# An attention kernel with a two-layer network behind it: ten and six tiles in two output halves, sums of q a unit ahead, and later places for some copies and adds

## The chip, the core and the metric

One Trainium2 chip, one of its cores. TensorE (PE) multiplies matrices, VectorE (DVE), ScalarE (ACT) and GpSimd (POOL) work on tiles, SyncE (SP) issues DMAs; each runs its own instructions in order, and semaphores join them. The metric is the device time of one execution in microseconds (us). Six runs of the kernel before gave 412.99 to 417.33, with a median of 413.75. Durations in the text come from one further execution with the profiler on.

## What is computed

```python
# q, k, v: (8, 12, 448, 64); x: (3584, 768); w_in: (768, 2048); w_out: (2048, 768)
q_n, k_n = rmsnorm(q, g_q), rmsnorm(k, g_k)
scores = matmul(q_n, k_n.transpose(0, 1, 3, 2)) / sqrt(64)
attn = exp(scores - max(scores)); attn = attn / (sum(attn) + 1e-9)
x = matmul(attn, v).transpose(0, 2, 1, 3).reshape(8 * 448, 768)
h = x @ w_in
out = maximum(0.01 * h, h) @ w_out
```

## The kernel before

**Units.** Attention runs in 24 units: 8 batches of 3 groups of 4 heads. For unit u, in this order and spread over several units' time: load q and k (`load`, by SP) and v (`load_v`, by GpSimd's queue); squares (`prep_sq` on ScalarE or `prep_sqp` on GpSimd, L148 and L152); their sums (`prep_ssq`, VectorE, L159); the reciprocal root in two small ScalarE steps (`prep_rinv`, L164 and L165); the normalised q and k in half precision (`prep_norm`, VectorE, L171); a transpose into qkT, on TensorE with VectorE copies for the first units (L753, L755) and by a DMA on SP's queue afterwards (`prep_trd`, L183); and then g's factor (`prep_g`, L155).

**A unit's own time** has four steps d. Step 0 scores column tile 0 (`score`, L199), steps 1 to 3 two tiles each. In step 0 VectorE takes the maximum (`shift_max`, L236) and builds dg (L238); TensorE then finishes the previous unit (products with v, L367, sums of exponentials, L307), and the two shift matmuls (L248) spread dg to all partitions; VectorE reduces them (L249) into the bias eb (L257), which every exponential of the unit needs (L218, ScalarE). Two slots in PSUM hold scores; each is free again when its exponential has been taken. The sums of exponentials are inverted by ScalarE (L327, L332), spread by four DMAs (rz, L337), and multiplied into x, by GpSimd (`xmul_pool`) or VectorE (`xmul_sb`), both at L347.

**The network** fills TensorE between the steps. `queue` holds its items, and `PLAN` says how many of them `fill` takes in each step. `moe1` makes one tile of 128 of the 2048 hidden columns from six matmuls (L389) and ScalarE's leaky step (L383). `moe2` makes half an output tile (384 columns) in two items of eight matmuls each (L435), copies it out of PSUM (VectorE, L439), and after the second half stores it (L409). From the second batch on, pairs of output tiles are made with seven products in place of eight (`seven`, items i0 to i6, L476): ma, mb, mc and md are PSUM banks, `sa` and `tw` hold sums of rows and of weights (`s1` to `s4`, `weight_sum`), and VectorE adds the products into the output tile (L483). i4 makes the fourth product in md, and i6 goes on accumulating in the same bank.

**What sets the order.** The program order is the order on each engine. `later` puts a step into `pend`; the next item's `flush` emits it. `fill` also emits one of the step's `jobs` (loads, sums, normalisation, transpose) after each item, and what is left of them at its end; in step 2 it skips that after an item that is marked `merges` (i4). At the end of step 3 `flush` keeps only s1 to s4 back, which come behind the next unit's maximum.

**The opening** (units 0 to 2, to about 43 us) is written out by hand, with `warm` matmuls between the steps. **The tail** multiplies the last batch's tiles; there (`mixed`) i0 puts half of mb's matmuls between ma's.

```python
flush(keep=d == 3 and u < NU - 1)          # at the end of fill
for i in range(8 * part, 8 * part + 8):    # moe2: two items of eight
```

Of the kernel before, what the change touches and what calls it, by code (L numbers as in the profile page):

```python
# [14 lines left out]
ds = bass.ds  # L15
# [3 lines left out]
def kernel(  # L19
# [11 lines left out]
    nc = tc.nc  # L31
# [6 lines left out]
    NU = B * NQ  # L38
# [28 lines left out]
    def drop(bank):  # L67
        if held:
            held[0].append(bank)
# [342 lines left out]
    pend = []  # L412
    L, R, LR = slice(0, HC), slice(HC, DM), slice(0, DM)

    def flush(keep=False):
        kept = [p for p in pend if keep and p[0] in (s1, s2, s3, s4)]
        now = [p for p in pend if p not in kept]
        pend[:] = kept
        for fn, args in now:
            fn(*args)  # L420
# [1 line left out]
    def out_tile():  # L422
        return opool.tile([P, DM], FP32, tag="ost", name="ost")

    def moe2(pair, t, half, part, late=False):
        flush()
        if half == 0 and part == 0:
            ost[0] = out_tile()
        if part == 0:
            ost[1] = aux([P, 512], FP32, "op2")  # L430
        op2 = ost[1]
        fts = (0, 1, 2, 3, 4, 5, 8, 9, 10, 12, 13, 11, 14, 15, 6, 7) if late else range(FT)
        for i in range(8 * part, 8 * part + 8):
            ft = fts[i]
            nc.tensor.matmul(op2[:, 0:HC], gt[:, ft, ds(col(t), P)], wout16[:, ft, ds(HC * half, HC)],  # L435
                             start=(i == 0), stop=(i == FT - 1))
        if part == 0:
            return
        nc.vector.tensor_copy(ost[0][:, ds(HC * half, HC)], op2[:, 0:HC])  # L439
        drop(op2)  # L440
        if half == 1:
            store(pair, t, ost[0], LR, False)

    def wblock(i, j):
        return wout16[:, HF * i:HF * i + HF, HC * j:HC * j + HC]
# [25 lines left out]
    def seven(pair, tt, nxt=None, last=False, mixed=False):  # L471
        g = {}

        def mm(bank, a, b, first, fs=range(HF)):
            for f in fs:
                nc.tensor.matmul(bank[:, 0:HC], a[:, f], b[:, f], start=(first and f == 0), stop=(f == HF - 1), skip_group_check=not first)  # L476

        def bank(name):
            g[name] = aux([P, 512], FP32, name)
            return g[name]  # L480

        def add(dst, src, name):
            nc.vector.tensor_tensor(dst, g[name][:, 0:HC], src, op=ALU.add)  # L483

        def put(i, c):
            store(pair, tt[i], g["o"][i], c, last)

        def i0():
            flush()
            g["o"] = (out_tile(), out_tile())  # L490
            ma = bank("ma")
            if mixed:
                mm(ma, gblock(tt[0], 0), wblock(0, 0), True, range(6))
                mm(bank("mb"), sa[:, 1], tw[:, 1], True, range(4))
            mm(ma, gblock(tt[0], 0), wblock(0, 0), True, range(6 if mixed else 0, HF))
            later(lambda: nc.vector.tensor_copy(g["o"][1][:, L], g["ma"][:, 0:HC]))

        def i1():
            flush()
            mm(g["mb"] if mixed else bank("mb"), sa[:, 1], tw[:, 1], True, range(4 if mixed else 0, HF))  # L500
            later(lambda: add(g["o"][1][:, L], g["o"][1][:, L], "mb"))
            later(lambda: drop(g["mb"]))

        def i2():
            flush()
            mm(g["ma"], gblock(tt[0], 1), wblock(1, 0), False)
            later(lambda: nc.scalar.copy(g["o"][0][:, L], g["ma"][:, 0:HC]))
            later(lambda: drop(g["ma"]))
            if last:
                later(put, 0, L)  # L510

        def i3():
            flush()
            mm(bank("mc"), sa[:, 0], tw[:, 0], True)
            later(lambda: add(g["o"][1][:, R], g["o"][1][:, L], "mc"))
            if nxt:
                later(s1, nxt)

        def i4():
            flush()  # L520
            mm(bank("md"), sa[:, 2], tw[:, 2], True)
            later(lambda: add(g["o"][1][:, R], g["o"][1][:, R], "md"))
            if last:
                later(put, 1, R)

        i4.merges = True

        def i5():
            flush()
            mm(g["mc"], sa[:, 3], wblock(1, 1), False)  # L530
            if nxt:
                later(s2, nxt)
            later(lambda: add(g["o"][0][:, R], g["o"][1][:, L], "mc"))
            later(lambda: drop(g["mc"]))
            later(put, 0, R if last else LR)
            if nxt:
                later(s3, nxt)
                later(s4, nxt)

        def i6():  # L540
            flush()
            mm(g["md"], gblock(tt[1], 1), tw[:, 3], False)
            later(lambda: add(g["o"][1][:, L], g["o"][1][:, L], "md"))
            later(lambda: drop(g["md"]))
            later(put, 1, L if last else LR)

        return [i0, i1, i2, i3, i4, i5, i6]

# [136 lines left out]
    def push(b):  # L685
        pair, odd = divmod(b, 2)
        fast = b > 0
        order = [f // 2 + HF * (f % 2) for f in range(FT)] if odd else range(FT)
        items = [(1.13, lambda ft=ft: (flush(), moe1(b, ft))) for ft in order]
        half = [(slice(0, 4)), (slice(4, 8))]  # L690
        late = b >= LATE
        after = {}
        if late:
            if odd:
                tt = (3, 4)
                for ns, f in (((1, 3), s1), ((4, 2), s2), ((3, 2), s3), ((5, 3), s4)):
                    after[ns] = [lambda f=f: f(tt, half[0])]
                after[3, 3] = [lambda f=f: f(tt, half[1]) for f in (s1, s2)]
            else:
                after[6, 2] = [lambda: win_sum(1, 0, (raws, "rq", 3))]  # L700
                after[1, 3] = [lambda: win_sum(2, 0, (raws, "rk", 3))]
                after[5, 2] = [lambda: win_sum(4, 0, (prep_p, "n16", 1))]
            item = late1(b, odd, after)
            fts = [0, 8, 1, 9, 2, 10, 3, 11]
            items = []
            for w in (LATE_ALL if odd else LATE_HALF):
                if w == "M":
                    items.append((1.13, lambda ft=fts.pop(0): (flush(), moe1(b, ft))))
                else:
                    items.append((0.575, lambda w=w: item(*w)))  # L710
        if odd:
            tt, tn = (3, 4), (5, 6)
            items += [(1.31, fn) for fn in seven(pair, tt, tn, mixed=late)]
            for n, x, fs in ((len(items) - 7, 1, (s3, s4)),) if late else ((8, 0, (s1, s2)), (10, 0, (s3, s4)), (FT - 1, 1, (s1, s2)), (FT, 1, (s3, s4))):
                c, fn = items[n]
                items[n] = (c, also(fn, *[lambda f=f, x=x: later(f, tt, half[x]) for f in fs]))
            items += [(1.31, fn) for fn in seven(pair, tn, None, b == B - 1)]
        else:
            tiles = (2,) if fast else (0, 1, 2)
            std = [lambda t=t, h=h, p=p: moe2(pair, t, h, p, late) for t in tiles for h in range(2) for p in range(2)]  # L720
            if fast:
                tt = (0, 1)
                std[0] = also(std[0], lambda: later(s1, tt), *[lambda: later(win_sum, 3, 0)] * late)
                std[1] = also(std[1], lambda: later(s2, tt))
                std[2] = also(std[2], lambda: later(s3, tt), lambda: later(s4, tt))
                std += seven(pair, tt)
            items += [(1.31, fn) for fn in std]
        queue.extend(items)
# [12 lines left out]
    def fill(u, d, jobs):  # L741
        for n in range(int(PLAN[u - 3][d])):
            fn = queue.pop(0)[1]
            fn()
            if jobs and not (d == 2 and hasattr(fn, "merges")):
                jobs.pop(0)()
        flush(keep=d == 3 and u < NU - 1)
        for job in jobs:
            job()

# [20 lines left out]
    with tc.manual_schedule():  # L771
# [72 lines left out]
        load(4)  # L844
        gate(1)
        prep_sqp(2, (1,))
        load_w_in(1024, 1024)
        wb = aux([P, 512], FP32, "warm")
        warm(12, wb)
# [9 lines left out]
        k1 = []  # L859
        tr(1, 1, ((K1, lambda *a: k1.append(a)),), tpk)  # L860
        score0(1)
        shift_max(1)
        vcopy(*k1[0])
        shift_bank(1)
# [4 lines left out]
        ex(0)  # L869
        warm(4, st[1]["pb"])  # L870
        shift_mm(1)
        prep_ssq(2)
        ex(1)
        qk(1, (1,))
        ex(1)
        zsum_slot(0)
        pv(0)
        prep_rinv(2)
        zinv(0)
        prep_norm(2)  # L880
        gate(2)
        prep_sqp(3)
        load_v(3)
        load(5)
        prep_sqp(4, (0,))
# [19 lines left out]
        shift_bank(2)  # L905
        warm(12, st[2]["pb"])
        shift_mm(2)
        prep_ssq(3)
        ex(2)
        qk(2, (1,))  # L910
        ex(2)
        zsum_slot(1)
        pv(1)
        prep_rinv(3)
        zinv(1)

        prep_norm(3)
# [11 lines left out]
        warm(8, st[2]["pb"])  # L929
        trn(3, 1, vcopy)  # L930
        xmul(1)
        prep_ssq(4)
        qk(2, (4,))
        ex(2)
        st[2]["zt"] = [aux([P, 512], FP32, "zt") for r in range(2)]
# [158 lines left out]
```

## Time and profile before

| | us |
|---|---|
| median of six runs | 413.75 |
| the profiled execution | 414.25 |
| its span, first to last instruction | 412.5 |
| TensorE busy | 398.2 |
| VectorE busy | 306.8 |
| ScalarE busy | 298.5 |
| GpSimd busy | 68.4 |
| DMA qkT<-n in the chain that ended last | 3.4% of the span |

The granted TensorE clock was 0.998. In the views, a row of the timeline has its start and length in us, the engine and line, the tile written and those read, the shape, a count of like instructions, and in brackets how long the engine was idle before, and for whom. The chain of waits is followed back from the last instruction, at each step to what released it.

### The profile page before, as it was taken

To read this page: it belongs to the slowest core of one execution; us is meant where nothing else is said; L and a number is where in the kernel's file an instruction comes from. 1 tells how busy PE (TensorE), PEld (TensorE's weight loads), DVE (VectorE), ACT (ScalarE), POOL (GpSimd) and SP (SyncE) were. 2 spreads that over 40 slices of the span, in tenths; PEclk is the share of its full clock that TensorE was granted. 3 is DMA by queue.
4 is the path that set the end of the run, shared out by engine and by line. 5 is a ranking of instruction groups with operands and counts; after the bars stand their busy time and mean duration, and the time that the engine had idled before them with its cause. 6 is when DMAs were issued, how large, how long until landed. Compare 5 with 4: busy or idle time off the path is not lost.

```text
span 412.5 us, 9399 instructions
## 1 busy us (share of the span) xinstructions
PE 398.2 (97%) x3840; PEld 219.1 (53%) x3840; DVE 306.8 (74%) x490; ACT 298.5 (72%) x470; POOL 68.4 (17%) x70
## 2 busy tenths in 40 slices
PE   8689999899999999999999999999999999999996
PEld 7445454454445544455445544454445557558953
DVE  5888889987988756767669757678568788658762
ACT  6898977577887689777986679966986657653600
POOL 1868442200020200020020200002001202000000
PEclk9999999999999999999999999999999999999999
DMA  6999999998565895577665796666562470032014
GB/s 205 276 237 252 242 229 247 209 181 187 147 157 86 220 236 106 156 195 162 157 152 80 211 208 138 164 145 158 186 114 46 121 151 17 9 78 76 2 40 114
DMA packets 72526, 62.87 MB, mean 152 GB/s; under 512 B 36388, under 2 KB 67620, under 8 KB 72484
## 3 DMA queue, kind: packets, MB, share of 16 engines
q1 hardware_dynamic: 61888, 50.08, 46.8%
q0 software_dynamic: 10272, 11.80, 18.8%
q8 instruction: 30, 0.49, 0.5%
q10 hardware_dynamic: 324, 0.39, 0.3%
q14 instruction: 12, 0.10, 0.1%
HBM read 45.61 MB, written 11.01 MB: 137 GB/s over the span
## 4 chain that ended last, share of the span: by engine, by line
PE 78%; DVE 10%; DMA 5%; ACT 3%; issue 2%; SPq 1%; DVEq 0%; ACTq 0%
PE hps L389 28%; PE sT L199 8%; PE sT L367 5%; PE bank L602 5%; PE bank L476 5%; PE mc L476 5%; PE ma L476 5%; PE md L476 4%; DMA qkT<-n 3%; DVE n L171 3%; PE op L435 2%; PE mb L476 2%; PE zc L307 2%; PE sT L476 1%; PE bank L435 1%
## 5 line engine op out<-in xcount | busy, mean ns | idle before, releaser
L218 ACT ACTIVATE et<-sT,eb 128x896 f16<-128x896 f32 x166 | 159.5, 1010 | 25.3 <-DVE eb L257 12.7
L389 PE MATMUL hps<-xt,win 128*128 128x448 f16 x600 | 120.8, 353 | 0.0
L389 PEld LDWEIGHTS <-win 128*128 128x128 f16 x612 | 56.7, 98 | 57.9 <-issue 9.9
L383 ACT ACTIVATE gt<-hps 128x448 f16<-128x448 f32 x100 | 53.8, 557 | 3.8 <-PE hps L389 3.2
L199 PE MATMUL sT<-qkT 64*64 64x448 f16 x664 | 52.5, 363 | 3.0 <-ACT et L218 2.1
L159 DVE TENSOR_REDUCE ssq<-sq 128x14 f32<-128x896 f32 (+2 forms) x49 | 50.1, 1058 | 0.6 <-ACT sq L148 0.6
L476 PEld LDWEIGHTS <-sa 128*128 128x128 f16 x352 | 32.8, 98 | 26.4 <-issue 5.8
L128 POOL DMA_DIRECT2D vt<-in_v_dram x24 | 17.9, 746 | 168.0 <-PE sT L367 167.7
L322 ACT COPY x<-sT 128x896 f32<-128x896 f32 x16 | 14.5, 906 | 30.0 <-DVE sT L249 30.0
L476 PEld LDWEIGHTS <-gt 128*128 128x128 f16 x264 | 25.3, 98 | 18.4 <-issue 2.1
L199 PEld LDWEIGHTS <-qkT 64*64 64x64 f16 x672 | 15.3, 104 | 36.1 <-issue 31.7
L347 POOL TENSOR_TENSOR xt<-x,rz 128x896 f16<-128x896 f32 x9 | 18.8, 2090 | 81.4 <-DMA rz<-zs 73.2
L367 PE MATMUL sT<-et,vt 64*64 64x448 f16 x560 | 29.9, 349 | 0.0
L171 DVE TENSOR_TENSOR n<-rq,rinv 128x896 f16<-128x896 f32 (+2 forms) x25 | 27.1, 1088 | 3.0 <-ACT rinv L165 3.0
L236 DVE TENSOR_REDUCE sT<-sT 128x1 f32<-128x896 f32 x22 | 24.1, 1094 | 6.2 <-PE sT L199 6.1
L435 PE MATMUL op<-wout,gt 128*128 128x384 f16 x160 | 28.4, 327 | 0.0
L292 DVE TENSOR_TENSOR ea<-ea,et 128x896 f16<-128x896 f16 x25 | 15.6, 625 | 14.4 <-ACT et L218 13.4
L171 DVE TENSOR_TENSOR n<-rk,rinv 128x896 f16<-128x896 f32 (+2 forms) x26 | 26.1, 1011 | 0.0
L367 PEld LDWEIGHTS <-vt 64*64 64x64 f16 x672 | 20.1, 107 | 10.8 <-issue 0.4
L435 PEld LDWEIGHTS <-gt 128*128 128x128 f16 x192 | 17.7, 98 | 13.7 <-issue 3.1
L476 PE MATMUL ma<-wout,gt 128*128 128x384 f16 x128 | 23.5, 326 | 0.0
L292 DVE TENSOR_TENSOR ea<-et 128x896 f16<-128x896 f16 x14 | 9.4, 672 | 11.4 <-ACT et L218 11.4
(144 smaller groups left out, 547.4 us busy)
## 6 DMA issues: line engine op xcount, KB each, us to landing
rq<-in_q_dram SPq DMA_DIRECT2D x24, 448.0 KB, 4.0
rk<-in_k_dram SPq DMA_DIRECT2D x24, 448.0 KB, 5.2
out_dram<-ost SPq DMA_DIRECT2D x52, 192.0 KB, 3.4
rz<-zs SPq DMA_DIRECT2D x80, 112.0 KB, 2.3
vt<-in_v_dram POOLq DMA_DIRECT2D x24, 224.0 KB, 5.6
win<-in_moe_w_in_dram POOLq DMA_DIRECT2D x8, 384.0 KB, 14.7
wout<-in_moe_w_out_dram POOLq DMA_DIRECT2D x2, 1536.0 KB, 27.8
out_dram<-ost SPq DMA_DIRECT2D x4, 96.0 KB, 2.1
```

The source lines that it names most:

```text
L159: nc.vector.tensor_reduce(buf(u, "ssq")[:, ti, :, c[0]:c[1]], buf(u, f"sq{ti}")[:, :, c[0]:c[1]], axis=AXL.X, op=ALU.add)
L171: nc.vector.tensor_tensor(buf(u, "n16")[:, ti, c[0]:c[1]].rearrange("p s a d -> p a s d"), src[:, :, c[0]:c[1]], buf(u, "rinv")[:, ti, :, ...
L199: nc.tensor.matmul(banks[a][64 * r:64 * r + 64, 0:S].rearrange("p (t x) -> p t x", t=NS), kT(u, r, a, t), qT(u, r, a), start=True, stop=True)
L218: nc.scalar.activation(s["et"][:, t], sT[:, :, 0:S], AF.Exp, bias=s["eb"], scale=1.0)
L236: nc.vector.tensor_reduce(s["spare"][:, 511:512], sT[:, :, 0:S], axis=AXL.XY, op=ALU.max)
L292: nc.vector.tensor_tensor(s["ea"], s["et"][:, 0] if t == 1 else s["ea"], s["et"][:, t], op=ALU.add)
L367: nc.tensor.matmul(s["pv"][r][64 * a:64 * a + 64, 0:S], vts[u % NV][64 * r:64 * r + 64, a, t], s["et"][64 * r:64 * r + 64, t, a], start=(t ...
L383: nc.scalar.activation(dst, src, AF.Prelu, bias=0.0, scale=1.0, alpha=0.01)
L389: nc.tensor.matmul(hps[:, 0:S], win16[:, kt // 2, kt % 2, ts(ft, P)], xt[:, kt // 2, kt % 2], start=(kt == 0), stop=(kt == KT - 1))
L435: nc.tensor.matmul(op2[:, 0:HC], gt[:, ft, ds(col(t), P)], wout16[:, ft, ds(HC * half, HC)], start=(i == 0), stop=(i == FT - 1))
L476: nc.tensor.matmul(bank[:, 0:HC], a[:, f], b[:, f], start=(first and f == 0), stop=(f == HF - 1), skip_group_check=not first)
L602: nc.tensor.matmul(bank[:, HX * i:HX * i + HX].rearrange("p (t x) -> p t x", t=NS), w, x[:, kt], start=start, stop=(kt == HK - 1), skip_gr ...
```

## The change

1. `moe2` has a parameter `cut`: for the second half of the first output tile and the first half of the third tile of batch 0, ten matmuls stand in the first item and six in the second.
2. For the first pair of batches, `moe2`'s copy and store go through `later`. At the end of step 3 of unit 5 they are kept back, and come behind unit 6's maximum.
3. In the opening, q's square and its sum for units 2, 3 and 4 are put a unit earlier, and `prep_rinv` goes ahead of an exponential and of the previous unit's products.
4. i6's add and store are kept back at the end of step 3, so they come behind the next unit's maximum.
5. A job is now also taken after i4, except in unit 12.
6. In the tail, half of mc's matmuls are put into i0, behind ma's.

The counts of instructions are the same on every engine. The order differs in these places:

- VectorE: q's sum of unit 2 stands ahead of unit 1's maximum, that of 3 ahead of unit 2's normalisation and that of 4 ahead of unit 3's; the copy ost<-op at the end of unit 5 stands behind dg of unit 6; the add ost<-md at the end of units 9, 12, 15, 18 and 21 stands behind dg of the next unit; in units 9, 15, 18 and 21 the normalisation of q stands ahead of the other add ost<-md.
- ScalarE: the rinv steps of units 2 and 3 stand ahead of an exponential.
- GpSimd: q's square of unit 3 stands ahead of four loads of w_in.
- SP: the loads of q and k in unit 6 stand ahead of two stores.
- TensorE: two matmuls L435 move over a score in units 5 and 6; four of L476 in the tail.

```diff
-    def flush(keep=False):
-        kept = [p for p in pend if keep and p[0] in (s1, s2, s3, s4)]
+    def flush(keep=0):
+        kept = [p for p in pend if keep and (p[0] in (s1, s2, s3, s4) or hasattr(p[0], "waits") or keep == 5 and hasattr(p[0], "copies"))]
...
-        for i in range(8 * part, 8 * part + 8):
+        for i in range(cut, FT) if part else range(cut):
...
-        nc.vector.tensor_copy(ost[0][:, ds(HC * half, HC)], op2[:, 0:HC])
-        drop(op2)
-        if half == 1:
-            store(pair, t, ost[0], LR, False)
+        o = ost[0]
+
+        def end():
+            nc.vector.tensor_copy(o[:, ds(HC * half, HC)], op2[:, 0:HC])
+            drop(op2)
+            if half == 1:
+                store(pair, t, o, LR, False)
+
+        end.copies = True
+        if pair == 0:
+            later(end)
+        else:
+            end()
...
             mm(ma, gblock(tt[0], 0), wblock(0, 0), True, range(6 if mixed else 0, HF))
+            if mixed:
+                mm(bank("mc"), sa[:, 0], tw[:, 0], True, range(4))
...
-            mm(bank("mc"), sa[:, 0], tw[:, 0], True)
+            mm(g["mc"] if mixed else bank("mc"), sa[:, 0], tw[:, 0], True, range(4 if mixed else 0, HF))
...
-            later(lambda: add(g["o"][1][:, L], g["o"][1][:, L], "md"))
-            later(lambda: drop(g["md"]))
-            later(put, 1, L if last else LR)
+            def end():
+                add(g["o"][1][:, L], g["o"][1][:, L], "md")
+                drop(g["md"])
+                put(1, L if last else LR)
+
+            end.waits = True
+            later(end)
...
-            std = [lambda t=t, h=h, p=p: moe2(pair, t, h, p, late) for t in tiles for h in range(2) for p in range(2)]
+            std = [lambda t=t, h=h, p=p: moe2(pair, t, h, p, late, 10 if not fast and (t, h) in ((0, 1), (2, 0)) else 8) for t in tiles for h in range(2) for p in range(2)]
...
-            if jobs and not (d == 2 and hasattr(fn, "merges")):
+            if jobs and not (d == 2 and u == 12 and hasattr(fn, "merges")):
                 jobs.pop(0)()
-        flush(keep=d == 3 and u < NU - 1)
+        flush(keep=u if d == 3 and u < NU - 1 else 0)
...
         prep_sqp(2, (1,))
+        prep_sqp(3, (0,))
         load_w_in(1024, 1024)
...
         score0(1)
+        prep_ssq(2, ALL, (0,))
         shift_max(1)
...
-        prep_ssq(2)
+        prep_ssq(2, ALL, (1,))
+        prep_ssq(3, ALL, (0,))
         ex(1)
+        prep_rinv(2)
         qk(1, (1,))
...
-        prep_rinv(2)
         zinv(0)
...
-        prep_sqp(3)
+        prep_sqp(3, (1,))
...
-        prep_ssq(3)
+        prep_ssq(3, ALL, (1,))
+        prep_ssq(4, ALL, (0,))
         ex(2)
+        prep_rinv(3)
         qk(2, (1,))
...
-        prep_rinv(3)
         zinv(1)
...
-        prep_ssq(4)
+        prep_ssq(4, ALL, (1,))
```

More of the change, by code (lines that the diff above doesn't have):

```diff
@@ L423, in out_tile, with moe2 @@
         return opool.tile([P, DM], FP32, tag="ost", name="ost")
-    def moe2(pair, t, half, part, late=False):
+    def moe2(pair, t, half, part, late=False, cut=8):
         flush()
```

## The prediction, made before the changed kernel had run

> **What bounds it now.** I read first the page's busy times, then TensorE's waits, then its timeline for where they lie, then the chain of waits and the timelines of the engines around each place.
>
> ```profile
> PE 398.2 (97%) x3840; PEld 219.1 (53%) x3840; DVE 306.8 (74%) x490; ACT 298.5 (72%) x470; POOL 68.4 (17%) x70
> ```
>
> TensorE is busy for all but 14 us of the span, and matmuls of one kind follow each other evenly (8 of 384 columns take 1.30 us, 0.163 each). The change removes no matmul, so it can win only idle time that the path meets.
>
> ```profile
> 82.46 0.22 PE L248 MATMUL sT<-dg,onesp 128*128 128x64 f16 x2 [0.97 <-DVE dg L238]
> 96.75 0.22 PE L248 MATMUL sT<-dg,onesp 128*128 128x64 f16 x2 [0.59 <-DVE dg L238]
> 284.79 0.22 PE L248 MATMUL sT<-dg,onesp 128*128 128x64 f16 x2 [0.33 <-DVE dg L238]
> 392.07 0.82 PE L476 MATMUL sT<-tw,sa 128*128 128x384 f16 x4 [0.16 <-DVE sa L460]
> ```
>
> Behind 43 us these are its idle gaps above 0.1 us: the maxima of units 6, 7 and 19, and the tail. Two short score waits (0.27 us, at 73.6 and 87.1) hide inside rows that count as busy.
>
> **Opening: about -0.21.** VectorE's normalisation of unit 3 (L171) waits for ScalarE's two small rinv steps, which stand behind an exponential:
>
> ```profile
> 31.97 0.32 ACT L164 ACTIVATE uu<-ssq,eps_t 128x28 f32<-128x28 f32 x1
> 32.58 1.09 DVE L171 TENSOR_TENSOR n<-rq,rinv 128x896 f16<-128x896 f32 x1 [0.64 <-ACT rinv L165]
> ```
>
> With q's sum a unit ahead, one sum (1.09) stands before rinv, not two, and rinv goes ahead of that exponential. Unit 2's normalisation starts 0.6 earlier, but the scores behind it still wait for exponentials on ScalarE, so its maximum gains 0.08. Unit 3's starts 0.7 earlier, at 31.85; but the exponential of step 1 is 0.4 later and with it the score that needs its slot (32.21 to 32.52); the twelve warm-up matmuls behind that, then the transposes, bring the second transpose to 34.56 (now 34.80), unit 3's k copy to 35.17 (35.38), the products of unit 1 0.22 earlier, and the last exponential of unit 2 to 38.27 (38.48). Everything to 54 us hangs on it: -0.21. Bounds: 0 if the slot wait eats it, -0.43 if all of ScalarE's idle time there goes. GpSimd's square moved ahead (1.69) delays four w_in issues; the earlier four still land until 31.7, the last of the moved ones at 42.2, and their first reader runs at 52.7: nothing. The extra sum in unit 1 fits a gap of 0.91 but for 0.05.
>
> **First batch: 0.** Unit 5's copy goes behind unit 6's maximum:
>
> ```profile
> 79.53 1.08 DVE L171 TENSOR_TENSOR n<-rk,rinv 128x896 f16<-128x896 f32 x1
> 80.53 0.55 DVE L439 COPY ost<-op 128x384 f32<-128x384 f32 x1
> 81.00 1.08 DVE L236 TENSOR_REDUCE sT<-sT 128x1 f32<-128x896 f32 x1
> ...
> 88.12 0.45 DVE L155 TENSOR_SCALAR qkT<-qkT,gcol 128x896 f16<-128x896 f16 x1 [1.38 <-DMA qkT<-n]
> ```
>
> The maximum starts 0.47 earlier and TensorE's 0.97 becomes 0.50. But the copy lands between it and L249, so exp's bias stays at 83.7. Above all VectorE next waits for unit 7's transpose, issued when the normalisation ended at 80.6, which does not move; from its landing VectorE runs without a pause to unit 7's maximum. The chain of waits says the same of units 6 and 7:
>
> ```profile
> 67.40 6.70 DMA qkT<-n
> ...
> 80.68 7.42 DMA qkT<-n
> ```
>
> So TensorE arrives at 96 us earlier by up to 0.47 and waits 1.0 for dg, not 0.59. What is late next is that transpose. The ten/six split: two matmuls (0.33) cover the 0.27 score wait. In unit 5 the score of step 3 is 0.3 later, its exponential too, and the slot for step 6 comes at 76.25, so the wait reappears there; in unit 6 it goes, into the same wait at 96. Bounds of this part: 0 to -1.56 (both gaps); a loss is excluded up to the 0.50 and 1.0 that TensorE waits there anyway; taken 0, because the landing is the row that ends last. The two loads moved ahead of the two stores on SP's queue are issued 1.3 earlier, before unit 8's transpose; VectorE waits for that at 101, TensorE doesn't.
>
> **Later merges: +1.19.** Two edits. (a) The last add of a group (md, 0.56) goes behind the next unit's maximum, five times. Only at 284.8 does TensorE wait for that maximum, because the add stands before it; the shift matmuls start 0.59 after their predecessor there, 0.19 in every unit without a wait: -0.40. Elsewhere TensorE's own scores come last: 0. (b) In units 9, 15, 18 and 21 q's normalisation goes ahead of the fourth product's add, so that add waits for rinv, for the normalisation and for what holds that; and the seventh product, which accumulates in the same bank, waits for the add. Unit 18 now:
>
> ```profile
> 277.56 0.56 DVE L483 TENSOR_TENSOR ost<-mc,ost 128x384 f32<-128x384 f32 x1 [0.67 <-PE mc L476]
> 278.87 0.56 DVE L483 TENSOR_TENSOR ost<-md,ost 128x384 f32<-128x384 f32 x1 [0.74 <-PE md L476]
> 279.34 1.94 DVE L171 TENSOR_TENSOR n<-rq,rinv 128x896 f16<-128x896 f32 x1
> ```
> ```profile
> 278.25 2.08 POOL L347 TENSOR_TENSOR xt<-x,rz 128x896 f16<-128x896 f32 x1 [8.22 <-ACT uu L164]
> ```
> ```profile
> 280.57 1.46 PE L476 MATMUL md<-tw,gt 128*128 128x384 f16 x8
> ```
>
> The normalisation took 1.94 instead of 1.08, and ended 0.95 after GpSimd's product (280.33); at 184.94 it took 1.23 and ended 0.95 after another. It was held until GpSimd was done. Moved, it is ready at 278.45 (rinv ends at 278.40), 0.2 after GpSimd started: it still ends at 281.28, the add at 281.76, and the seventh product starts at 281.8 instead of 280.57: +1.24, with which the -0.40 is still earned, since the maximum then has time. Unit 9:
>
> ```profile
> 137.69 2.08 POOL L347 TENSOR_TENSOR xt<-x,rz 128x896 f16<-128x896 f32 x1 [8.54 <-DMA rz<-zs]
> ```
>
> Ready at 138.78, held to 139.77, done at 140.72, add done at 141.19, product at 141.25 instead of 140.90: +0.35. Units 15 and 21: GpSimd ends at 232.63 and 327.42, before rinv (233.13, 327.91); the add ends 0.6 before the product: 0. So 1.24 + 0.35 - 0.40 = +1.19; bounds -0.40 (never held) to +5.2 (four times 1.4, when GpSimd starts just before each).
>
> The Trainium skill, SBUF — State Buffer, section "SBUF: two separate sides", calls the port pair shared by VectorE and GpSimd an exclusive lock, taken by whichever starts first, also for a VectorE operation with two SBUF inputs against a GpSimd one that reads SBUF. The rows above show it with GpSimd first; no row shows VectorE first, where by that page this order would cost nothing in unit 18 and the sum of this part would be -0.05.
>
> **Tail: -0.32.** Four products of mc (4 x 0.163 = 0.65) are put before mb's second half, which starts 0.48 after its predecessor, 0.32 more than 0.163; their sums are ready since 384.7. Bounds 0 and -0.32.
>
> **Sum.** -0.21 + 0 + 1.19 - 0.32 = +0.66. The profiled execution took 414.25 (span 412.5 and 1.75 around it), so 414.9 for it; it lay 0.5 above the median of the six runs, 413.75, so I forecast 414.4.
>
> **Rivals.** (1) No hold: rz, which GpSimd's product waits for, lands 0.2 later in unit 18, so that VectorE goes first there, and 0.35 earlier in unit 9. For: the margin of 0.2. Against: in units 12, 15 and 21 GpSimd starts 4.8 after zs's exponential, in unit 18 5.5, and the normalisation is ready at 5.7. -0.21 - 0.40 - 0.32 = -0.93: 412.8. (2) The first batch does pay: the transposes land earlier (they take 6.7 and 7.4 against a median of 4.1 while the DMA engines are at 90% or more), and up to 1.5 of the waits at 82 and 96 go; with (1), 411.3, alone 412.9. Against: their issue doesn't move. (3) Slower: rz lands as late as in unit 9 or later in units 15 and 21 as well. The hold reaches TensorE from GpSimd starting 6.0 after zs's exponential (now 4.8) and costs up to 1.4 at 7.4; 1.0 in each, with unit 9 at 1.0 too, gives 414.4 + 2.65 = 417.0. For: unit 9 has 6.3 already. Against: 4.8 in both others. (4) The opening earns nothing or its gain is lost at the transposes: 414.6, within the forecast's spread.
>
> **Numbers.** Forecast with (4) 0.6, (1) 0.2, (2) 0.1, (3) 0.1. About 0.5% (2.07 us) is what a measurement of this kernel tells from no change: below 411.7 is faster, above 415.8 slower. The forecast gives 0.02 to slower, (1) 0.02 to faster, (2) 0.06 to faster, (3) 0.07 to slower. The range leaves out the far halves of (2) and (3) and some of the scatter of runs (412.99 to 414.68 but for one): 411.9 to 415.6. The forecast's own is 413.6 to 415.2.
>
> **What would show it.** Right: gaps at 82 near 0.5 and at 96 near 1.0; L171 in unit 18 above 2.5 us, with a wait of TensorE for the md add of L483 above 1 us; no gap at 285 or at 392. Wrong: L171 at 1.08 there and no such wait; a gap at 96 below 0.5; transposes landing earlier than 74.1 and 88.1.

## The result and the profile after

The changed kernel took 414.55 us (median of 28 runs, 412.39 to 420.42), the kernel before 414.25 in the 63 runs taken beside it. The ratio is 0.9997, 95% interval 0.9975 to 1.0018: no difference that can be measured. The forecast was 414.4 and "the same". In both kernels about a third of the runs lie 3 to 4 us above the others (20 of 63 from 415.94 up, 9 of 28 from 416.67 up), so the medians say little about less than 1 us. Parts of the change do move time, in both directions, and the experiments separate them.

The profiled execution took 415.49 (span 413.7) against 414.25 (412.5). In the changed code L476 has become L485, L483 has become L492, L439 L442, and the copies L753 and L755 are L768 and L770. TensorE's timeline after, at the places that were shown for before:

```profile
83.36 0.22 PE L248 MATMUL sT<-dg,onesp 128*128 128x64 f16 x2 [0.53 <-DVE dg L238]
...
97.10 0.22 PE L248 MATMUL sT<-dg,onesp 128*128 128x64 f16 x2
...
282.53 1.46 PE L485 MATMUL md<-tw,gt 128*128 128x384 f16 x8 [1.18 <-DVE ost L492]
...
286.35 0.23 PE L248 MATMUL sT<-dg,onesp 128*128 128x64 f16 x2
...
393.32 1.46 PE L485 MATMUL sT<-tw,sa 128*128 128x384 f16 x8
```

The gap at unit 6 is halved (0.97 to 0.53), those at unit 19 and in the tail are gone, that at unit 7 is down to 0.15, and a new one of 1.18 stands ahead of the seventh product of unit 18, which waits for VectorE's md add (L492). VectorE's timeline there says why:

```profile
279.05 2.96 DVE L171 TENSOR_TENSOR n<-rq,rinv 128x896 f16<-128x896 f32 x1 [0.31 <-ACT rinv L165]
281.94 0.54 DVE L492 TENSOR_TENSOR ost<-md,ost 128x384 f32<-128x384 f32 x1
```

and GpSimd's, in the same microseconds:

```profile
278.99 2.07 POOL L347 TENSOR_TENSOR xt<-x,rz 128x896 f16<-128x896 f32 x1 [8.34 <-DMA rz<-zs]
```

GpSimd started 0.06 before the normalisation of q, which then took 2.96 instead of 1.08 and ended 0.95 after GpSimd's product. The md add behind it started at 281.94, where TensorE had been free since 281.35.

It helps to cut each execution into stages, by the starts of TensorE's first product of hidden columns (L389) and of the shift matmuls of a unit. "Start" is the time of the first exponential, which hangs on the first loads alone. Every stage that is left out is equal within 0.03 in all profiles, but for 0.20 more at units 7 to 8 and 0.25 more at 12 to 13 in the kernel without eight warm-ups.

| profile | start | opening: start to first L389 | first L389 to unit 7 | unit 9 to 10 | unit 18 to 19 | unit 23 to start of last matmul |
|---|---|---|---|---|---|---|
| before | 12.25 | 31.04 | 53.46 | 16.11 | 15.37 | 55.77 |
| before, second profile | 12.38 | 31.66 | 52.11 | 16.11 | 15.85 | 55.77 |
| changed | 13.20 | 31.09 | 52.81 | 16.38 | 16.31 | 55.45 |
| changed, second profile | 12.75 | 31.08 | 51.82 | 16.98 | 16.34 | 55.45 |
| changed without part 5 | 12.46 | 31.10 | 51.82 | 16.11 | 14.96 | 55.46 |
| the same, second profile | 12.38 | 31.89 | 51.82 | 16.11 | 14.97 | 55.45 |
| changed, GpSimd later in units 9, 18 | 12.47 | 31.09 | 51.82 | 16.11 | 14.96 | 55.46 |
| parts 1, 2 alone | 13.20 | 31.03 | 51.81 | 16.11 | 15.62 | 55.78 |
| part 3 alone | 12.86 | 32.21 | 51.80 | 16.11 | 15.47 | 55.77 |
| parts 4, 6 alone | 12.87 | 31.99 | 51.81 | 16.11 | 15.05 | 55.45 |
| part 5 alone | 12.41 | 31.51 | 51.86 | 17.01 | 15.51 | 55.78 |
| before, a v load later | 12.41 | 31.04 | 53.54 | 16.11 | 15.60 | 55.78 |
| changed without part 5, 8 warm-ups less | 12.39 | 30.63 | 52.30 | 16.11 | 15.40 | 55.45 |
| changed without part 5, 20 less | 12.86 | 30.35 | 56.14 | 16.11 | 14.96 | 55.44 |

From the first row to the third: 0.95 from the first loads, +0.05 in the opening, -0.65 in the first batch, +0.27 at unit 9, +0.94 at unit 18, -0.32 in the tail.

### The profile page after: what moved, and what is told of

Read it like the earlier page. It is cut to its first block, busy times and chain, and to the rows that moved or that the text cites. A ratio compares the mean times of both kernels' runs of the same rounds, so it can differ in the third digit from the quotient of the medians.

```text
span 413.7 us, 9395 instructions
## 1 busy us (share of the span) xinstructions
PE 399.1 (96%) x3840; PEld 220.7 (53%) x3840; DVE 308.7 (75%) x490; ACT 298.3 (72%) x470; POOL 68.3 (17%) x70
## 4 chain that ended last, share of the span: by engine, by line
PE 85%; DVE 6%; ACT 4%; issue 2%; DMA 2%; DVEq 0%
PE hps L389 28%; PE sT L199 9%; PE sT L367 6%; PE ma L485 5%; PE bank L485 5%; PE bank L617 5%; PE md L485 4%; PE op L435 4%; PE mc L485 4%; ACT et L218 3%; PE mb L485 3%; PE zc L307 2%; PE warm L784 2%; PE sT L485 2%; DMA qkT<-n 2%
## 5 line engine op out<-in xcount | busy, mean ns | idle before, releaser
L389 PE MATMUL hps<-xt,win 128*128 128x448 f16 x600 | 120.8, 353 | 0.0
L389 PEld LDWEIGHTS <-win 128*128 128x128 f16 x612 | 56.7, 98 | 57.9 <-issue 9.9
L485 PEld LDWEIGHTS <-sa 128*128 128x128 f16 x352 | 32.9, 98 | 25.9 <-issue 5.8
L485 PEld LDWEIGHTS <-gt 128*128 128x128 f16 x264 | 25.3, 98 | 20.0 <-issue 3.9
L171 DVE TENSOR_TENSOR n<-rq,rinv 128x896 f16<-128x896 f32 (+2 forms) x25 | 29.0, 1162 | 3.3 <-ACT rinv L165 3.3
L367 PE MATMUL sT<-et,vt 64*64 64x448 f16 x560 | 29.9, 349 | 0.0
L435 PE MATMUL op<-wout,gt 128*128 128x384 f16 x160 | 28.4, 327 | 0.0
L367 PEld LDWEIGHTS <-vt 64*64 64x64 f16 x672 | 20.2, 107 | 10.6 <-issue 0.4
L435 PEld LDWEIGHTS <-gt 128*128 128x128 f16 x192 | 17.7, 98 | 13.7 <-issue 3.1
L485 PE MATMUL ma<-wout,gt 128*128 128x384 f16 x128 | 23.5, 326 | 0.0
```

The costliest lines, as they stand in the source:

```text
L171: nc.vector.tensor_tensor(buf(u, "n16")[:, ti, c[0]:c[1]].rearrange("p s a d -> p a s d"), src[:, :, c[0]:c[1]], buf(u, "rinv")[:, ti, :, ...
L367: nc.tensor.matmul(s["pv"][r][64 * a:64 * a + 64, 0:S], vts[u % NV][64 * r:64 * r + 64, a, t], s["et"][64 * r:64 * r + 64, t, a], start=(t ...
L389: nc.tensor.matmul(hps[:, 0:S], win16[:, kt // 2, kt % 2, ts(ft, P)], xt[:, kt // 2, kt % 2], start=(kt == 0), stop=(kt == KT - 1))
```

## The experiments

The theory after the result: part 5 (a job after i4) puts the normalisation of q ahead of the md add, where GpSimd's product holds it; this costs about what parts 4 and 6 earn, and the opening and the first batch earn nothing of their own. The rivals: the loss at unit 18 comes from the later adds of part 4; or parts 1 to 3 pay, and something else takes it back.

**Without part 5.** Expected:

> The changed kernel without edit 5: q's normalisation stands behind the add of the fourth product again, everything else as changed. Theory (the add waits for a normalisation that GpSimd holds): TensorE's waits for the md add in units 9 and 18 (0.27 and 1.34 us in the profile after) are gone, the normalisation of q in unit 18 may still take up to 1.9 us, and no wait for dg comes at unit 19; the time is 1.6 below the changed kernel, about 0.7 below the kernel before. Rival (the two waits only take the place of others that are late anyway): the time stays within 0.3 of the changed kernel and a wait of about 1 us shows at unit 19's maximum.

```diff
-            if jobs and not (d == 2 and u == 12 and hasattr(fn, "merges")):
+            if jobs and not (d == 2 and hasattr(fn, "merges")):
```

Measured: 412.92 us, ratio to before 0.9959 (0.9921 to 0.9998). No wait for the md add, unit 9 as before, unit 18 shorter by 0.41 than in the first profile of before. VectorE in unit 18:

```profile
277.50 0.56 DVE L492 TENSOR_TENSOR ost<-md,ost 128x384 f32<-128x384 f32 x1 [0.74 <-PE md L485]
277.98 2.08 DVE L171 TENSOR_TENSOR n<-rq,rinv 128x896 f16<-128x896 f32 x1
```

The normalisation is still held (2.08), but stands behind the add; of what TensorE needs next, only the maximum of unit 19 is behind it. So part 5 is the loss, and part 4 is not. Behind the add the hold still has a price: in the kernel before, with the normalisation at 1.94 and 2.42 in its two profiles, the stage took 15.37 and 15.85; with part 4 there is more room, and it took 15.05 at 2.28 (parts 4 and 6 alone) and 15.40 at 2.63 (without eight warm-ups).

**Part 5 alone, on the kernel before.** Expected:

> The kernel before with edit 5 alone. Theory: waits of TensorE for the md add of about 0.3 in unit 9 and 1.2 to 1.4 in unit 18, the gap at unit 19's maximum (0.33 to 0.40) gone; span 1.1 to 1.3 above the kernel before, counted from the first exponential. Rival (no hold, or the wait is cover): within 0.3 of it, gap at unit 19 kept.

```diff
-            if jobs and not (d == 2 and hasattr(fn, "merges")):
+            if jobs and not (d == 2 and u == 12 and hasattr(fn, "merges")):
```

Measured: 414.88 us, ratio 1.0015 (0.9985 to 1.0046). Unit 9 lost 0.90, more than expected; TensorE there:

```profile
140.85 1.46 PE L476 MATMUL md<-tw,gt 128*128 128x384 f16 x8 [0.74 <-DVE ost L483]
```

Unit 18 did not lose the 1.2 to 1.4 expected, and the gap at unit 19 stayed (0.48). It showed what no profile had shown: VectorE came first. Its timeline,

```profile
278.39 1.09 DVE L171 TENSOR_TENSOR n<-rq,rinv 128x896 f16<-128x896 f32 x1 [0.31 <-ACT rinv L165]
279.40 0.55 DVE L483 TENSOR_TENSOR ost<-md,ost 128x384 f32<-128x384 f32 x1
279.87 2.51 DVE L171 TENSOR_TENSOR n<-rk,rinv 128x896 f16<-128x896 f32 x1
```

and GpSimd's:

```profile
278.46 2.97 POOL L347 TENSOR_TENSOR xt<-x,rz 128x896 f16<-128x896 f32 x1 [8.48 <-ACT rinv L165]
```

With VectorE ahead by 0.07, q's normalisation took its 1.09, GpSimd's product 2.97 instead of 2.08, and the normalisation of k, behind it, was held instead (2.51, again to 0.95 after GpSimd's end). The md add was in time. A lead of a few hundredths of a microsecond (0.06 and 0.03 for GpSimd in the two profiles of the changed kernel, 0.07 for VectorE here) decided which of the two paid. That the loss of unit 18 is there in one execution of the same kernel and not in another would follow, but isn't shown: both profiles of the changed kernel have it.

**GpSimd's product behind both normalisations, in units 9 and 18 of the changed kernel.** Expected:

> The changed kernel, but in units 9 and 18 GpSimd's product starts only after both normalisations (a one-element copy of GpSimd from the normalised tile stands ahead of it). The order on VectorE is that of the changed kernel. Theory (an exclusive hold by GpSimd): q's normalisation takes 1.08 in both units, the md add follows in time, no wait of TensorE for it; 1.6 below the changed kernel, like the version without edit 5. Rival (rinv or the order on VectorE alone is to blame, GpSimd is not): the waits of 0.3 and 1.3 us stay, the time stays that of the changed kernel.

```diff
-                if d == 1 and narrow(u - 1) and not 5 <= u < 8 and ADDED.get(u, 0) < 4:
+                if d == 1 and narrow(u - 1) and not 5 <= u < 8 and ADDED.get(u, 0) < 4 and u not in (9, 18):
...
+                        if u in (9, 18):
+                            job(gate, u + 2)
+                            job(xmul_pool, u - 1)
```

Measured: 412.76 us, ratio 0.9965 (0.9945 to 0.9986). VectorE's order is that of the changed kernel; only GpSimd's place is another. VectorE, unit 18:

```profile
277.09 1.09 DVE L171 TENSOR_TENSOR n<-rq,rinv 128x896 f16<-128x896 f32 x1 [0.31 <-ACT rinv L165]
278.10 0.55 DVE L492 TENSOR_TENSOR ost<-md,ost 128x384 f32<-128x384 f32 x1
```

GpSimd:

```profile
279.72 0.18 POOL L260 COPY gate_t<-n 128x1 f16<-128x1 f16 x1 [11.04 <-DVE n L171]
279.98 2.09 POOL L347 TENSOR_TENSOR xt<-x,rz 128x896 f16<-128x896 f32 x1
```

The normalisation is back at 1.09, and units 9 and 18 take 16.11 and 14.96, as without part 5. The hold is the cause, not the place of the normalisation by itself.

**Parts 1 and 2 alone.** Expected:

> The kernel before with edits 1 and 2 alone (ten and six, copy behind unit 6's maximum). Theory (VectorE and the transposes set the end of units 5 and 6): the gap at unit 6's maximum falls by 0.4 to 0.5, and what is won there is lost at unit 7's maximum, unless unit 7's transpose lands in less than the 7.4 us of before; from unit 5's maximum to unit 7's shift matmuls 29.4 us, as before, if that transpose takes 7.4, and one us less for each us that it is shorter. Rival (the edit itself pays): 0.6 less between these points with a transpose of 7.4.

```diff
+        kept = [p for p in pend if keep and (p[0] in (s1, s2, s3, s4) or keep == 5 and hasattr(p[0], "copies"))]
...
+        for i in range(cut, FT) if part else range(cut):
```

(An excerpt; the copy and store through `later` are as in the change.) Measured: 413.81 us, ratio 0.9971 (0.9947 to 0.9996). First L389 to unit 7: 51.81, 1.65 less than in the first profile of before. By itself this looked like a gain. Unit 7's transpose was short here, so that the case of the expectation (a transpose of 7.4) did not come up.

**The kernel before and the changed kernel, profiled a second time.** Expected:

> The kernel before, unchanged, profiled once more. Theory (in the first batch the landing of unit 7's transpose sets the end, and it varies between executions by itself): if that transpose lands in 4 to 5 us here, the gaps at the maxima of units 6 and 7 shrink to below 0.6 together and unit 7's shift matmuls come 1 to 1.6 earlier, counted from the first exponential, than in the first profile (84.5). Rival (edits 1 and 2 pay): the transpose takes 7.4 again, the gaps are 0.97 and 0.59 again, 84.5.

> The changed kernel, unchanged, profiled once more. Theory (GpSimd's hold): TensorE's waits for the md add are 0.3 to 0.8 in unit 9; in unit 18 either about 1.3 (GpSimd's product starts first) or none (VectorE's normalisation starts first, and then GpSimd's product is drawn out to some 3 us instead of 2.08, as in the run of edit 5 alone), nothing between. Rival (the wait is a property of the order alone): 1.2 to 1.4 in unit 18 every time. Tail and unit 19: no gaps.

Measured: before 413.86 us, ratio to its other runs 0.9993 (0.9972 to 1.0014); changed 413.76, ratio 0.9972 (0.9938 to 1.0007). The kernel before now had 52.11 from the first L389 to unit 7 without any edit, the changed one 51.82: most of the 1.65 isn't the edit's. The hold of the changed kernel was as in its first profile (normalisation 3.00 in unit 18, TensorE's gap 1.22), and larger at unit 9 (+0.87, not +0.27). VectorE, GpSimd and TensorE in unit 18:

```profile
278.22 3.00 DVE L171 TENSOR_TENSOR n<-rq,rinv 128x896 f16<-128x896 f32 x1 [0.31 <-ACT rinv L165]
```
```profile
278.19 2.08 POOL L347 TENSOR_TENSOR xt<-x,rz 128x896 f16<-128x896 f32 x1 [8.38 <-ACT rinv L165]
```
```profile
281.74 1.46 PE L485 MATMUL md<-tw,gt 128*128 128x384 f16 x8 [1.22 <-DVE ost L492]
```

**Part 3 alone (the opening).** Expected:

> The kernel before with edit 3 alone (the opening). Theory (the second transpose of unit 3 waits for the warm-up matmuls' last write, since it gets their bank): from the first exponential to the first matmul of the network 31.1 us, as in the profile after (31.09) and before (31.03), within 0.1; the transpose starts 0.67 after the first of the eight warm-up matmuls ahead of it. Rival (my step: it was unit 3's normalisation that it waited for): 30.8.

```diff
         score0(1)
+        prep_ssq(2, ALL, (0,))
         shift_max(1)
...
+        prep_rinv(2)
         qk(1, (1,))
```

(An excerpt; the edit is the whole of part 3.) Measured: 413.74 us, ratio 0.9998 (0.9975 to 1.0021); opening 32.21. Inconclusive by itself: the granted clock was 0.86 between 7 and 31 us in this execution, and in every profile with a clock below 1.00 there the opening was longer (0.93: 31.66; 0.94: 31.89; 0.86: 32.21 and 31.99). Among those at 1.00, four with part 3 have 31.08 to 31.10, three without it 31.03 and 31.04 (part 5 alone, 31.51, is left out: there q of unit 2 came late, and GpSimd's square of it held a normalisation to 1.61). Part 3 earns nothing: +0.05.

**The kernel before, with the v load behind unit 7's transpose held back.** Expected:

> The kernel before, but in unit 6 GpSimd first copies one column of that unit's bias, so the load of v that it issues there (0.35 us behind unit 7's transpose in the first profile) comes some 3 us behind the transpose. Theory (the two share the DMA engines, and the transpose takes 6.4 to 7.4 with a load of v right behind it, 4.2 to 4.6 with 1.3 us or more between them): unit 7's transpose is issued by SP in 1.3 and lands in 4.0 to 4.6; unit 7's shift matmuls 1 to 1.6 us earlier from the first exponential than in the first profile (84.5), time 1 to 1.5 below the kernel before where that has the slow transpose. Rival (the load has nothing to do with it): transpose as in the other run of the kernel before in this call.

```diff
+                        if u == 6:
+                            nc.gpsimd.tensor_copy(gate_t, st[u]["eb"])
                         load_v(u + 3)
```

Measured: 413.77 us, ratio 0.9986 (0.9966 to 1.0006). The expected gain of 1 us and more didn't come (53.54). Unit 7's transpose itself did get short, 4.5 against 7.42, but unit 6's took longer here (7.46 until VectorE's next step, against 6.72), and the gap of 1.14 that this left at unit 6 kept the stage long.

**Without the eight, and without twenty, of the warm-up matmuls around unit 3's transposes; parts 4 and 6 alone; and the kernel without part 5 again.** Expected:

> The changed kernel without the moved normalisation, and without the eight warm-up matmuls that stand between unit 3's two groups of transposes in the opening. Theory (the opening earned nothing because TensorE runs these warm-ups in the order written, so that the normalisations, done early, are not used): from the first exponential, the second group of transposes starts 0.6 us earlier than with them, VectorE's copy of k about 0.4 earlier (it then follows the copy of q at once, and VectorE's wait of 0.37 for the transposes is gone), the first product of hidden columns 0.3 to 0.4 earlier; the time 0.3 below that of the same kernel with them. Rival 1 (something else, the exponentials on ScalarE, sets the end of the opening): the first product of hidden columns not earlier by 0.1. Rival 2 (the warm-ups keep the clock up): the granted clock falls in this stage and the opening gets longer.

> As the one before, and the twelve warm-up matmuls ahead of unit 3's transposes are left out as well. Theory: the transposes follow the normalisations, k's copy starts 1.0 us earlier from the first exponential than with all twenty, ScalarE's two short waits for scores in unit 2 (0.29 and 0.43) go, and the first product of hidden columns comes 0.4 to 0.7 earlier; the time 0.5 below that of the same kernel with them. Rival 1 (ScalarE sets the end): no more than with the eight gone. Rival 2 (clock): the granted clock falls below 1.0 between 32 and 45 us and the stage gets longer.

> The kernel before with only two parts of the change: the last add of a group behind the next unit's maximum, and the four products of mc ahead of mb's second half in the tail. Theory: TensorE's gap at unit 19 (0.33 to 0.8 in the profiles of the kernel before) goes, the tail's wait of 0.32 goes, everything up to unit 18 is as before; ratio to before 0.9970 to 0.9985. Rival (the normalisation of q and the maximum of unit 19 come no earlier without the moved normalisation, because VectorE is late anyway): only the tail's 0.32 goes, ratio 0.9992.

> The changed kernel without the moved normalisation, a second time, as the basis for the two without warm-ups. It gave 412.9 us and a ratio of 0.9959 (0.9921 to 0.9998). Expected 0.995 to 0.998 again, with a transpose of unit 7 of 4 to 5 us, no wait of TensorE for the md add, and no idle gap of TensorE above 0.15 us behind 45 us but for late first loads.

The edit for "without twenty" (for "without eight" only the second `warm` goes; both stand on the kernel without part 5):

```diff
-        warm(12, st[2]["pb"])
         qk(2, (3,))
         ex(2)
         trn(3, 0, vcopy)
-        warm(8, st[2]["pb"])
         trn(3, 1, vcopy)
```

| | median | ratio to before |
|---|---|---|
| without part 5 | 412.87 | 0.9950 (0.9926 to 0.9974) |
| and without 8 warm-ups | 412.89 | 0.9960 (0.9928 to 0.9992) |
| and without 20 | 414.73 | 1.0001 (0.9968 to 1.0034) |
| parts 4 and 6 alone | 413.36 | 0.9983 (0.9951 to 1.0014) |

Parts 4 and 6 alone (their lines are those of the change) do what they were expected to: unit 18 takes 15.05 against 15.37 and 15.85 of before, the tail 55.45 against 55.77; the gain is there in the stages, though the interval of the ratio still reaches 1. The kernel without part 5 has no wait of TensorE behind 45 us in its second profile but one of 0.42 for a score in unit 5, which had not been expected here.

The opening behaves as the theory has it. TensorE in the changed kernel:

```profile
34.73 0.56 PE L179 MATMUL tp<-ident,n 128*128 128x128 f16 x7
35.13 0.61 PE L784 MATMUL pb<-onesp 128*128 128x128 f16 x8
35.80 0.55 PE L179 MATMUL tp<-ident,n 128*128 128x128 f16 x7
```

and VectorE, which has finished the normalisation of k at 34.71 and waits for TensorE:

```profile
33.63 1.08 DVE L171 TENSOR_TENSOR n<-rk,rinv 128x896 f16<-128x896 f32 x1
35.34 0.68 DVE L768 TENSOR_SCALAR qkT<-tp,gcol 128x896 f16<-128x896 f16 x1 [0.62 <-PE tp L179]
36.39 0.62 DVE L770 COPY qkT<-tp 128x896 f16<-128x896 f16 x1 [0.37 <-PE tp L179]
```

Without the eight, TensorE makes all fourteen transposes at one go,

```profile
33.93 0.96 PE L179 MATMUL tp<-ident,n 128*128 128x128 f16 x14
```

and the opening is 0.47 shorter (30.63); without the twenty, 0.75 (30.35); the granted clock stays at 1.00 from 7 to 45 us in both. Yet the time doesn't follow. Without the eight, the first batch and unit 18 give it all back (52.30 and 15.40, where the kernel with them has 51.82 and 14.97). Without the twenty, the twelve runs fall into two groups, six from 412.22 to 413.32 and six from 416.13 to 418.59. The profile is of the upper group, and TensorE waits in the first batch:

```profile
95.55 0.54 PE L389 MATMUL hps<-xt,win 128*128 128x448 f16 x2 [2.16 <-DVE xt L347]
...
99.35 0.22 PE L248 MATMUL sT<-dg,onesp 128*128 128x64 f16 x2 [0.84 <-DVE dg L238]
```

VectorE there waits 3.91 for unit 7's transpose, which landed 9.49 after its issue. GpSimd had issued a v load 0.17 after it. SP's queue and GpSimd's in this profile:

```profile
81.22 1.32 SPq L183 DMA_TRANSPOSE qkT<-n  x1
```
```profile
81.39 0.76 POOL L128 DMA_DIRECT2D vt<-in_v_dram  x1 [3.52 <-PE sT L367]
```

and in the second profile of before:

```profile
80.73 1.32 SPq L183 DMA_TRANSPOSE qkT<-n  x1
```
```profile
81.78 0.76 POOL L128 DMA_DIRECT2D vt<-in_v_dram  x1 [4.40 <-PE sT L367]
```

The fourteen profiles side by side:

| | unit 6, issue to VectorE's L155 | v load behind unit 7's transpose | unit 7's transpose, to landing |
|---|---|---|---|
| 20 warm-ups less | 7.34 | 0.17 | 9.49 |
| changed | 7.08 | 0.32 | 6.41 |
| before | 6.72 | 0.35 | 7.42 |
| 8 warm-ups less | 6.72 | 0.68 | 6.24 |
| nine others | 5.73 to 6.20 | 1.05 to 1.43 | 4.2 to 4.8 |
| before, v load held back | 7.46 | 3.69 | 4.5 |

The v load is released by TensorE (sT L367), the transpose by VectorE. When unit 6's transpose is slow, VectorE is late, the next transpose is issued just ahead of the v load, and it is slow too. The last row breaks this: unit 6 as slow as ever, the load out of the way, and the transpose takes 4.5. It is one execution, and the distance to the load isn't the whole rule: unit 6's own transpose always has the next v load 1.50 behind it, and where VectorE waits for it (eleven profiles) it takes 5.97 to 7.46. Why unit 6's transpose is slow in some executions stays open. The four profiles with a late opening and a low clock have 5.73 to 6.15, the ten others 5.77 to 7.46, as if an early one met loads that are still under way; no run tried this.

The table also tells what parts 1 and 2 are worth when both transposes are slow. In its first four rows VectorE waits for both. Their stages from the first L389 to unit 7 (56.14, 52.81, 53.46, 52.30) less the two times of the table leave 39.31 to 39.34, in the kernel before as in the three with parts 1 and 2. So the stage follows the transposes there, and the edits earn nothing; the -0.65 of the changed kernel is +0.36 for unit 6's transpose and -1.01 for unit 7's.

**The best version** is the changed kernel without part 5: medians of 412.92 and 412.87, both intervals below 1. The kernel before had 414.25 and 414.1 beside it; the changed kernel, at other times, 414.55 and 413.76. Parts 1 and 2 alone also have an interval below 1 (to 0.9996, ten runs) though their stages show no gain; this stays open.

## Why the prediction was right, and where it was not

- **Sum.** +0.66 was forecast for the profiled execution. The stages give +0.29 (0.05 - 0.65 + 0.27 + 0.94 - 0.32), and the first loads another 0.95, which is no part of the change. The time forecast holds; two terms of the sum don't, and their misses have opposite signs (+0.26 in the opening, -0.65 in the first batch). That 414.4 lies so near to 414.55 is partly luck: it was worked out from a median of 413.75, and beside the changed kernel the kernel before had 414.25. The medians moved by +0.30, and the interval of the ratio, -1.0 to +0.7 us, can't tell that from the +0.66.
- **Later merges, +1.19: right.** Measured +0.27 at unit 9 (0.35 forecast) and +0.94 at unit 18 (1.24 - 0.40 = 0.84 forecast): +1.21. The mechanism is shown by three runs: without part 5 the wait goes, with GpSimd out of the way it goes, and part 5 alone brings it at unit 9. Units 15 and 21 lost nothing, as forecast. The single sizes scatter (unit 9 lost 0.27, 0.87 and 0.90 in three profiles), so that the two agree to 0.02 is luck.
- **The rival without a hold was half right.** Its condition, VectorE first in unit 18, came in one profile of three in which part 5 stands with GpSimd's product in its old place, by 0.07: that of part 5 alone, not of the changed kernel, and with unit 9 still held. The Trainium skill, SBUF — State Buffer, section "SBUF: two separate sides", says that whichever starts first has the shared port pair for its whole instruction; the trace now agrees in both directions (VectorE 2.96 instead of 1.08 behind GpSimd, GpSimd 2.97 instead of 2.08 behind VectorE).
- **Tail, -0.32: right,** in all profiles with part 6 (55.77 to 55.45).
- **Opening, -0.21: wrong,** +0.05, as the fourth rival had it. The step that failed is "bring the second transpose to 34.56 (now 34.80)". I took the transpose to follow the normalisation, which in before ends 0.13 ahead of it. But the eight warm-ups between unit 3's two groups of transposes, 0.67 from their start to that of the second group, end at the same moment, and they didn't move earlier (34.13 in before, 35.13 less 0.95 for the later start in after): the score ahead of them waits for the exponential that rinv now precedes. Taking them out shortened the opening by 0.47.
- **First batch, 0: right as the effect of the edits, wrong as the reading of the profile.** The forecast wait of 1.0 at unit 7 was 0.15, "a gap at 96 below 0.5", which was named as a sign of error. The failed step is "VectorE next waits for unit 7's transpose, issued when the normalisation ended at 80.6, which does not move": I took the 7.42 of one execution for a property of the kernel. Without the edits it takes 4.2 to 4.8 in four other profiles (the one with the v load held back aside), and the stage is then 51.80 to 52.11; with the edits and short transposes it is 51.81 or 51.82. Where both transposes are slow, the remainder of 39.3 is the same with and without the edits. The score wait that the ten/six split covers comes back as one of 0.42 in unit 5, as forecast.

So the change has one sound gain (parts 4 and 6: -0.32 in the tail, -0.41 to -0.89 at unit 18 where the hold is short), and part 5 takes it back: 1.35 at unit 18 (16.31 against 14.96) and 0.27 to 0.87 at unit 9. In the profiles it takes more than that: units 9 and 18 and the tail together are 0.9 above the kernel before in the first pair of profiles and 1.0 in the second, which the intervals of the two ratios (up to +0.7 and +0.3 us) don't reach. Both profiled executions of the changed kernel, 415.49 and 414.72, lie 0.9 to 1.0 above the medians of its runs, so a typical run loses less than these profiles show. That VectorE comes first at unit 18 in those runs would fit, but none of them was profiled.

## What to carry to other kernels

Before an operation of VectorE is moved ahead of one that TensorE waits for, look at what GpSimd runs in the same microseconds: where one holds the other, as here, the later one pays the whole rest of the earlier, and so does everything queued behind it. A single long DMA or a single gap in one profile isn't a property of the kernel; take a second profile of the unchanged kernel before you price an edit by it. Where an engine starts an operation just when its operand is ready, check what else ends at that moment on its own queue, because removing one of two limits that coincide earned nothing here.

## What the runs showed of the hardware

- A normalisation that is held by GpSimd's product ended 0.95 after it each time (unit 18 in the changed kernel twice, and 0.96 without part 5; the one of k with part 5 alone): it does nearly all of its 1.08 after the release. Adds of VectorE that read PSUM (L483, 0.55 beside GpSimd's product) were not held.
- Unit 7's DMA transpose took 6.2 to 9.5 with another queue's load issued within 0.7 of it, and 4.2 to 4.8 with the load 1.05 behind or more, in all fourteen profiles. It isn't a rule for every transpose: unit 6's took 5.97 to 7.46 in eleven profiles with the load 1.50 behind.
- The granted clock between 7 and 31 us was 0.86 to 0.94 in four of fourteen profiles, of kernels with and without the edits, and the opening was longer by 0.6 to 1.1 in these; what lowers it stays open. The window's rows for the kernel without part 5, and for parts 4 and 6 alone (time, then busy time of each engine, clock, DMA share, GB/s):

```profile
7.00:31.00 24.00, 18.43 (x281) 11.98 (x282) 22.02 (x41) 21.30 (x32) 18.32 (x22) 1.00 1.08 270
```
```profile
7.00:31.00 24.00, 19.66 (x261) 12.99 (x261) 19.79 (x36) 20.47 (x30) 14.96 (x19) 0.86 1.06 262
```
